# Eight W1 units started on two token tiles, with the other two tiles loaded through a transposing DMA

## The chip, the cores and the metric

One Trainium2 chip; the kernel runs on one of its cores. The metric is the device time of one execution in microseconds, as the median of several runs. A profiled execution beside them gives the span (first to last instruction), what every engine did, and when each DMA landed.

The engines are written as the profile writes them: PE (TensorE, matmul), PEld (its weight loads), ACT (ScalarE), DVE (VectorE), POOL (GpSimd) and SP (SyncE, which only issues DMAs here). ACT issues DMAs too.

## The reference

Two branches read the same input x (2048 tokens by 512) and are mixed by a gate. `B_x` is not used.

```
x = A_x
g = _sigmoid((x * gate_w).sum(-1, keepdims=True))

# A: linear attention, 32 heads of 16
qkv = x @ wqkv                                   # 512 -> 3 * 512
pq, pk = q @ w_phi, k @ w_phi                    # per head, 16 x 16
phi = concatenate([softmax(p), softmax(-p)])     # per head, 32 features
kv = einsum("bhsf,bhsd->bhfd", phi_k, v);  z = phi_k summed over the tokens
o  = (phi_q @ kv) / (phi_q . z + 1e-6)
a  = o @ wo

# B: dense layer with relu
b = maximum(x @ w1, 0) @ w2                      # 512 -> 1376 -> 512

return g * a + (1 - g) * b
```

## The kernel before

**Tiles.** The 2048 tokens are 16 tiles of 128, or four chunks of 512. The contraction over 512 is done in four row blocks j of 128. `XT` holds x transposed (features on the partitions), `W1` the first dense weight by row blocks, `HT` the hidden layer after the relu. The 1376 hidden columns are ten units of 128 and a rest of 96 which also carries the gate's column.

**Tasks and orders.** The program is a graph of named tasks. Each has an engine, a function that emits instructions, and the tasks that it waits for. The order of the tasks on each engine is written out by hand in the table `ORDER` (lines 17 to 62), one string for each engine; `schedule` only checks it. The numbers `dur`, `lat` and `boost` of a task are not used for the order. `settle` leaves out waits that others imply, and `emit` writes the instructions. Each DMA has a semaphore of its own.

The names that matter here:

- `x00` to `x03`: plain loads of the first four tiles of x, 128 KB each; `xt..` transposes one on PE against the identity (lines 382 to 391), two blocks at a time; `xe..` evicts the result from PSUM to `XT`, on ACT (L396) and DVE (L399).
- `w1a0` to `w1a3`: the columns 0 to 511 of W1, one row block each, 128 KB. `w1b`: columns 512 to 1023, all row blocks, 512 KB. `w1c`: the rest. All are issued at L306, on SP or ACT.
- `hh..`: the first four W1 units on tiles 0 and 1 (256 tokens), row block by row block, as the loads land (L439). `hr..` and the first `h0_0` to `h0_3`: the same units on tiles 2 and 3 (L445). Then `h0_4` and so on: a unit on a whole chunk of 512 tokens, four matmuls of 512 columns (L425).
- `rl..`: relu of a unit from PSUM into `HT`, on ACT (L503).
- `wphi`, `wbd..`, `wkT`, `f1_..` (L408), `fe1_..`: the head-wise map is folded into the key weight; the evictions `fe1_..` alternate between DVE (L378) and ACT (L376).
- `pr_k0` to `pr_k8` (L545): keys of two tiles at a time, features already mapped; `ev` (ACT, L577) evicts, `mx` and `mn` (DVE) reduce, `t1` and `t2` (POOL, L590) subtract, `ex` (ACT, L595) takes the exponential, `sm` and `rc` (DVE) sum and invert, `nm` (POOL, L604) normalises. `pr_q..` does the same for the queries (`ra` and `nm` on POOL, L623 and L627).
- `v..` (L526) and `kv..` (L611): the values, and phi_k times v summed over all tiles. `kv15` is the last one; `kn` and `kz` then evict the sum.
- `nd..` (L654), `to..`, `a..` (L682) and `b..` (L676): numerator and denominator, the transposed result, and the two output projections. Most of this fills the last third.
- `x1`, `x2`, `x3`, `wkT`, `wqT`: transposing loads (`load_t`, L311) on SP. `x1` waits until `w1c` has landed.
- `warm0`: six matmuls on constants at the start (L292).

PSUM has eight banks: 3, 4, 5 (`HB`) and 2 for the W1 units, 0, 1, 6 and 7 (`FB`) for the transposes, the folds, and later for other work. A bank's next user waits for its last eviction (`freed`).

Of the kernel before, what the change touches and what calls it, by code (L numbers as in the profile page):

```python
# [5 lines left out]
ACT = mybir.ActivationFunctionType  # L6
# [176 lines left out]
def bass_gated_mix__linear_kernel_hedgehog__dense_activation_relu__prompt_kernel(  # L183
# [38 lines left out]
    with ExitStack() as es:  # L222
# [157 lines left out]
        XB, FB = ((0, 1), (6, 7), (0, 1), (6, 7)), (0, 1, 6, 7)  # L380
# [7 lines left out]
        for m in range(4):  # L388
            for n in range(2):
                add(f"xt{m}{n}", "pe", lambda q, m=m, n=n: pe_xt(q, m, n),  # L390
                    (f"x0{m}", "ident", f"xe{m - 2}{n}" if m > 1 else None), dur=0.2, boost=9000.0 - 10 * m)
            for n, eng in enumerate(("act", "dve")):
                xo = XT[:, 2 * n:2 * n + 2, m * P:(m + 1) * P]
                xi = PS[:, XB[m][n], 0:2 * P].rearrange("p (j t) -> p j t", j=2)
                if eng == "act":
                    add(f"xe{m}{n}", eng, lambda q, o=xo, i=xi: q.activation(o, i, ACT.Copy), (f"xt{m}{n}",), dur=0.35,  # L396
                        boost=9000.0 - 10 * m)
# [15 lines left out]
        for c in range(NC):  # L413
            units += [("h", c, k) for k in range(KT - 1)]
# [5 lines left out]
        freed[FB[2]] = ("xe30",)  # L420
        w1of = {k: (() if k < 4 else ("w1b",) if k < 8 else ("w1c",)) for k in range(KT)}
# [15 lines left out]
        def pe_h_first(q, j, c0, c1, ks=range(4)):  # L437
            for k in ks:
                last = q.matmul(PS[:, GB4[k], c0:c1], W1[:, j, k * P:(k + 1) * P], XT[:, j, c0:c1],  # L439
# [3 lines left out]
        def pe_h_rest(q, k, c0, c1, first):  # L443
            for j in range(ND):
                last = q.matmul(PS[:, GB4[k], c0:c1], W1[:, j, k * P:(k + 1) * P], XT[:, j, c0:c1],  # L445
                                start=(j == 0 and first), stop=(j == ND - 1), skip_group_check=True)
# [7 lines left out]
        for n, (j, ks) in enumerate(((1, range(4)), (2, range(4)), (3, (0, 1)), (3, (2, 3)))):  # L454
            add(f"hh{n + 1}", "pe", lambda q, j=j, ks=ks: pe_h_first(q, j, 0, 2 * P, ks),
                (f"xe0{j // 2}", f"xe1{j // 2}", f"w1a{j}", prev), dur=0.11 * len(ks), boost=8500.0)
            prev = f"hh{n + 1}"

        for k in range(2):
            add(f"hr{k}", "pe", lambda q, k=k: pe_h_rest(q, k, 2 * P, 3 * P, True), ("xe20", "xe21", prev), dur=0.22,  # L460
                boost=8200.0)
            prev = f"hr{k}"
        for line in (("warm0", "xt00", "xt01", "xt10", "xt11", "hh00", "hh01", "hh1", "hh2", "xt20", "xt21", "hh3", "xt30", "xt31",
                      "hh4", "hr0", "hr1"), ("xe00", "xe10", "xe20", "xe30"),
                     ("ident", "shift", "xe01", "xe11", "xe21", "xe31", "blk", "row4", "mk")):
# [10 lines left out]
        for n, (kind, a, k) in enumerate(units):  # L476
            b = GB4[n] if n < 4 else FB[2] if n == 4 else HB[(n - 4) % len(HB)]
            if kind == "h":
                halved = n < 4
                deps = [*xof[a], *w1of[k], prev, *freed[b]]  # L480
                if k == KT - 1:
# [298 lines left out]
```

## Time and profile before

| what | us |
|---|---|
| median of 3 runs (150.11 to 150.15) | 150.13 |
| the profiled execution | 149.87 |
| its span | 148.3 |
| PE busy | 145.5 (98%) |
| DVE busy | 111.7 (75%) |
| POOL busy | 109.6 (74%) |
| ACT busy | 91.4 (62%) |

The share of busy time says who works, not who sets the end. For that the profile follows a chain back from the last instruction, at each step to what released it. A matmul's end is modelled, and matmuls overlap, so how fast PE works is read from the distance of their starts. For a DMA the profile gives the issue on the engine's queue and the time from the issue to the landing.

Landings of the early loads, issue and landing in us from the start of the span:

| load | issued | landed |
|---|---|---|
| x00 (SP), x01 (ACT) | 0.74, 0.74 | 3.45, 3.64 |
| w1a0 (SP), w1a1 (ACT) | 1.20, 1.18 | 4.12, 4.33 |
| w1a2 (SP), w1a3 (ACT) | 1.66, 1.67 | 4.83, 5.10 |
| x02, x03 (SP) | 2.13, 2.60 | 5.37, 5.68 |
| w1b, wphi (SP) | 3.08, 3.55 | 7.56, 7.79 |
| wkT, w1c, wv (SP) | 4.11, 7.43, 8.05 | 9.46, 11.54, 12.92 |

### The profile page before, as it was taken

The page shows a single profiled execution, that of the slowest core. Times are in us where ns is not written, and L with a number is a line of the kernel's source. Part 1 is how long each engine was busy: PE and PEld are TensorE (multiplying, and loading weights), DVE is VectorE, ACT ScalarE, POOL GpSimd, SP SyncE. Part 2 cuts the span into 40 slices and gives each one's busy share as a digit, 9 for nine tenths or more (in the row PEclk, how much of TensorE's full clock was granted, in tenths as well). Part 3 has the DMA queues.
Part 4 walks back from the last instruction along what each step waited for, and adds up shares of the span by engine and source line. Part 5 has one row for each costly group of instructions (what it writes and reads, how often), then busy time and mean ns, then how long its engine had stood idle before and what let it go on. Part 6 is the DMA issues. An engine that isn't in the chain of part 4 may idle for free.

```text
span 148.3 us, 2542 instructions
## 1 busy us (share of the span) xinstructions
PE 145.5 (98%) x1009; PEld 75.3 (51%) x1009; DVE 111.7 (75%) x169; ACT 91.4 (62%) x126; POOL 109.6 (74%) x72
## 2 busy tenths in 40 slices
PE   7999999999999999999999999999999999999994
PEld 2875444445654475445444545455444444445453
DVE  2433666998896948989999997999999988634502
ACT  3475769799969765898983937175583751310141
POOL 4000499999999999999999999999999793150000
PEclk9999999999999999999999999999999999999999
DMA  4998999910040001000000093646957785556752
GB/s 139 324 256 220 169 187 214 340 51 4 0 73 0 0 4 38 0 0 4 0 0 0 7 141 71 141 95 138 183 119 167 180 214 116 141 134 158 64 157 92
DMA packets 46363, 16.11 MB, mean 109 GB/s; under 512 B 39856, under 2 KB 46352, under 8 KB 46352
## 3 DMA queue, kind: packets, MB, share of 16 engines
q1 hardware_dynamic: 43760, 13.61, 42.6%
q10 hardware_dynamic: 2592, 2.34, 4.9%
q8 instruction: 8, 0.13, 0.4%
q14 instruction: 3, 0.02, 0.1%
HBM read 4.41 MB, written 2.10 MB: 44 GB/s over the span
## 4 chain that ended last, share of the span: by engine, by line
PE 98%; DVE 0%; issue 0%
PE PS L676 24%; PE PS L425 21%; PE PS L545 19%; PE PS L526 9%; PE PS L682 9%; PE PS L611 3%; PE PS L654 3%; PE PS L433 2%; PE PS L292 2%; PE PS L698 2%; PE PS L439 2%; PE PS L445 1%; PE PS L408 1%; PE PS L384 1%; PE PS L709 1%; DVE OSB L719 0%
## 5 line engine op out<-in xcount | busy, mean ns | idle before, releaser
L590 POOL TENSOR_TENSOR TS<-PB,MX 128x1024 bf16<-128x1024 bf16 (+1 forms) x18 | 30.9, 1723 | 14.5 <-DVE MX L581 14.5
L676 PE MATMUL PS<-W,HT 128*128 128x512 bf16 (+1 forms) x165 | 38.1, 379 | 0.0
L597 DVE TENSOR_REDUCE ZB<-FT 128x128 f32<-128x2048 bf16 (+1 forms) x18 | 36.6, 2031 | 1.8 <-ACT FT L595 1.8
L595 ACT ACTIVATE FT<-TS 128x2048 bf16<-128x2048 bf16 (+1 forms) x18 | 30.9, 1718 | 9.6 <-POOL TS L590 9.5
L425 PE MATMUL PS<-XT,W 128*128 128x512 bf16 x144 | 34.7, 379 | 0.0
L590 POOL TENSOR_TENSOR TS<-MN,PB 128x1024 bf16<-128x1024 bf16 (+1 forms) x18 | 30.9, 1726 | 0.8 <-DVE MN L583 0.8
L545 PE MATMUL PS<-WP,XT 128*128 128x512 bf16 x128 | 30.6, 379 | 0.0
L604 POOL TENSOR_TENSOR FT<-FT,SC 128x2048 bf16<-128x2048 bf16 (+1 forms) x9 | 29.6, 3293 | 0.0
L503 ACT ACTIVATE HT<-PS 128x512 bf16<-128x512 f32 x40 | 22.6, 597 | 5.4 <-PE PS L425 4.6
L581 DVE TENSOR_REDUCE MX<-PB 128x64 bf16<-128x1024 bf16 (+1 forms) x18 | 19.5, 1085 | 5.9 <-ACT PB L577 5.9
L676 PEld LDWEIGHTS PS<-W,HT 128*128 128x128 bf16 (+1 forms) x165 | 15.4, 98 | 16.9
L730 ACT ACTIVATE OSB<-PS,OMG 128x512 bf16<-128x512 f32 x14 | 9.6, 686 | 21.1 <-PE PS L682 20.5
L583 DVE TENSOR_REDUCE MN<-PB 128x64 bf16<-128x1024 bf16 (+1 forms) x18 | 19.3, 1084 | 3.2 <-ACT PB L577 3.2
L425 PEld LDWEIGHTS PS<-XT,W 128*128 128x128 bf16 x144 | 13.7, 98 | 15.4
L577 ACT ACTIVATE PB<-PS 128x1024 bf16<-128x1024 f32 (+1 forms) x18 | 16.7, 927 | 7.2 <-PE PS L545 4.0
L545 PEld LDWEIGHTS PS<-WP,XT 128*128 128x128 bf16 x128 | 12.1, 98 | 13.5
L526 PE MATMUL PS<-WV,XT 128*128 128x512 bf16 x64 | 16.4, 379 | 0.0
L627 POOL TENSOR_TENSOR FT<-FT,SR 128x1024 bf16<-128x1024 bf16 (+1 forms) x9 | 15.7, 1740 | 0.7
L682 PE MATMUL PS<-WO,OT 128*128 128x512 bf16 x60 | 14.9, 378 | 0.0
L663 DVE SCALAR_TENSOR_TENSOR OTM<-PS,EG,RD 128x256 bf16<-128x256 f32 x32 | 13.8, 463 | 0.2
L661 DVE RECIPROCAL RD<-PS 128x16 f32<-128x16 f32 x32 | 6.4, 232 | 9.0 <-PE PS L654 8.8
L535 ACT ACTIVATE VS<-PS 128x512 bf16<-128x512 f32 x16 | 9.6, 602 | 4.3 <-PE PS L526 4.3
(55 smaller groups left out, 106.6 us busy)
## 6 DMA issues: line engine op xcount, KB each, us to landing
out_dram<-OSB ACTq DMA_DIRECT2D x14, 128.0 KB, 2.2
W<-in_B_w_dram SPq DMA_DIRECT2D x1, 1280.0 KB, 7.5
W<-in_B_w_dram SPq DMA_DIRECT2D x1, 512.0 KB, 4.5
WV<-in_A_wqkv_dram SPq DMA_DIRECT2D x1, 512.0 KB, 4.9
WO<-in_A_wo_dram SPq DMA_DIRECT2D x1, 512.0 KB, 7.5
FT<-in_A_x_dram SPq DMA_DIRECT2D x3, 128.0 KB, 3.1
W<-in_B_w_dram SPq DMA_DIRECT2D x1, 352.0 KB, 4.1
W<-in_B_w_dram ACTq DMA_DIRECT2D x2, 128.0 KB, 3.3
```

The lines of the kernel that those rows point to most:

```text
L425: last = q.matmul(PS[:, b, :], W1[:, j, k * P:(k + 1) * P], XT[:, j, chunk(c)], start=(j == 0), stop=(j == ND - 1))
L503: add(f"rl{a}_{k}", "act", lambda q, a=a, k=k, b=b: q.activation(HT[:, k, chunk(a)], PS[:, b, :], ACT.Relu), (prev,), dur=0.6, boost=RL)
L526: last = q.matmul(PS[:, 2, :], XT[:, j, m * P:(m + 1) * P], WV[:, j, :], start=(j == 0), stop=(j == ND - 1))
L545: last = q.matmul(PS[:, n, :], XT[:, j, m * P:(m + 1) * P], WP[:, s, j, :], start=(j == 0), stop=(j == ND - 1))
L581: add(f"mx_{J}", "dve", lambda q, sl=sl, w=w, i=pbg: q.tensor_reduce(MX[:, sl, 0:w * H], i, AX.X, ALU.max), (f"ev_{J}", old("t1")), dur=0. ...
L583: add(f"mn_{J}", "dve", lambda q, sl=sl, w=w, i=pbg: q.tensor_reduce(MN[:, sl, 0:w * H], i, AX.X, ALU.min), (f"ev_{J}", old("t2")), dur=0. ...
L590: add(f"{tn}_{J}", "pool", lambda q, o3=o3, a3=a3, b3=b3: q.tensor_tensor(o3, a3, b3, ALU.subtract), (f"{'mx' if sg == 0 else 'mn'}_{J}", ...
L595: add(f"ex_{J}", "act", lambda q, fs=fs, ts=ts, w=w: q.activation(FT[:, fs, 0:w * F], TS[:, ts, 0:w * F], ACT.Exp), (f"t1_{J}", f"t2_{J}", ...
L597: add(f"sm_{J}", "dve", lambda q, fs=fs, sl=sl, w=w: q.tensor_reduce(ZB[:, sl, 0:2 * w * H], FT[:, fs, 0:w * F].rearrange("p (g d) -> p g ...
L604: add(f"nm_{J}", "pool", lambda q, f3=f3, sl=sl, w=w: q.tensor_tensor(f3, f3, SC[:, sl, 0:2 * w * H].unsqueeze(2).to_broadcast([P, 2 * w * ...
L676: last = q.matmul(PS[:, ab, :], HT[0:r, k, m * P:(m + 1) * P], W2[0:r, k, :], start=(k == 0), stop=False)
L682: last = q.matmul(PS[:, ab, :], OT[:, m % NOT, t, :], WO[:, t, :], start=False, stop=(t == ND - 1))
```

## The change

- Tiles 2 and 3 of x are no longer loaded plainly and transposed on PE. One transposing load, `x0b`, brings them straight into `XT`. It stands on SP behind `wphi` and ahead of `wkT`. The tasks `x02`, `x03`, `xt2.`, `xt3.`, `xe2.`, `xe3.` are gone.
- `w1b` is split into `w1b0` (row blocks 0 and 1, on SP, where `x02` was) and `w1b1` (row blocks 2 and 3, on ACT), 256 KB each.
- Eight W1 units, not four, are started on tiles 0 and 1, by row blocks: `hh00` to `hh3` for units 0 to 3 and `hg0` to `hg3` for units 4 to 7, in the banks 3, 4, 5, 2, 0, 1, 6, 7 (`GB8`). Their second halves (tiles 2 and 3) follow in the order 4 to 7, then 0 to 3, each four matmuls of 256 columns. The folds `f1_..` take banks 0, 1, 6, 7 and so wait for the relus of units 4 to 7.
- The relus of units 1, 5 and 7 of the first chunk go from ACT to DVE, as a maximum with 0.
- A small activation, `first`, stands on ACT between the issue of `x01` and that of `w1a1`.
- The orders on all engines are new up to about `kv15`; from there on they are the same.

```diff
-        load_x(0, "sp", 2.95)
-        load_x(1, "act", 3.1)
-        load_w(0, "sp", 3.2)
-        load_w(1, "act", 3.4)
-        load_w(2, "sp", 3.8)
-        load_w(3, "act", 3.95)
-        load_x(2, "sp", 4.0)
-        load_x(3, "sp", 3.9)
-        load("w1b", "sp", W1[:, :, 512:1024], w1r[:, :, 512:1024], dur=0.5, lat=5.0)
+        load_x(0, "sp", 2.95)
+        load_x(1, "act", 3.1)
+        add("first", "act", lambda q: q.activation(EP[:, 0:1], bass.AP(tensor=one, offset=0, ap=[[1, P], [1, 1]]), ACT.Copy),
+            (), dur=1.5)
+        after_last("first", "act")
+        for j in range(ND):
+            load(f"w1a{j}", ("sp", "act")[j % 2], W1[:, j, 0:512], w1r[:, j, 0:512], dur=0.45, lat=3.3)
+        for j in range(2):
+            load(f"w1b{j}", ("sp", "act")[j], W1[:, 2 * j:2 * j + 2, 512:1024], w1r[:, 2 * j:2 * j + 2, 512:1024], dur=0.45, lat=3.9)
         load("wphi", "sp", WPS[:, :, :], A_w_phi.rearrange("(g hl) r c -> (hl r) g c", g=ND), dur=0.5, lat=4.9)
+        load_t("x0b", XT[:, :, 2 * P:4 * P], x2[2 * P:4 * P, :], (), 1.3, 2.5)
         load_t("wkT", WT[:, ND:2 * ND, :], A_wqkv[:, D:2 * D], (), 4.1, 2.7)
...
-        def pe_h_rest(q, k, c0, c1, first):
+        def pe_h_rest(q, k, c0, c1):
             for j in range(ND):
-                last = q.matmul(PS[:, GB4[k], c0:c1], W1[:, j, k * P:(k + 1) * P], XT[:, j, c0:c1],
-                                start=(j == 0 and first), stop=(j == ND - 1), skip_group_check=True)
+                last = q.matmul(PS[:, GB8[k], c0:c1], W1[:, j, k * P:(k + 1) * P], XT[:, j, c0:c1],
+                                start=(j == 0), stop=(j == ND - 1), skip_group_check=True)
             return last
-        GB4 = (*HB, 2)
+        GB8 = (*HB, 2, *FB)
...
+        for j in range(1, ND):
+            add(f"hh{j}", "pe", lambda q, j=j: pe_h_first(q, j, 0, 2 * P),
+                (f"xe0{j // 2}", f"xe1{j // 2}", f"w1a{j}", prev), dur=0.44, boost=8500.0)
+            prev = f"hh{j}"
+        for j in range(ND):
+            add(f"hg{j}", "pe", lambda q, j=j: pe_h_first(q, j, 0, 2 * P, range(4, 8)),
+                ("xe00", "xe01", "xe10", "xe11", f"w1b{j // 2}", prev), dur=0.44, boost=8500.0)
+            prev = f"hg{j}"
...
+                if a == 0 and k in (1, 5, 7):
+                    add(f"rl{a}_{k}", "dve", lambda q, a=a, k=k, b=b: q.tensor_scalar(
+                        HT[:, k, chunk(a)], PS[:, b, :], 0.0, None, ALU.max), (prev,), dur=0.69, boost=RL)
+                else:
+                    add(f"rl{a}_{k}", "act", lambda q, a=a, k=k, b=b: q.activation(
+                        HT[:, k, chunk(a)], PS[:, b, :], ACT.Relu), (prev,), dur=0.6, boost=RL)
...
-            war = [f"xe{2 + j // 2}{j % 2}"] + (["rl0_4"] if j == 2 else [])
+            war = [f"rl0_{4 + j}"]
```

The new orders, up to the first key maximum on each engine, and on POOL and PE up to `nm_k8` and `kv15`:

```
sp    x00 w1a0 w1a2 w1b0 wphi x0b wkT w1c wv x1 x2 wqT x3 gw w2a w2b wo ...
act   x01 first w1a1 w1a3 w1b1 xe00 xe10 rl0_4 rl0_6 fe1_1 fe1_3 rl0_2 ev_k0 rl0_3 rl0_0 rl0_8 ...
dve   ident shift xe01 xe11 blk row4 wbd1 wbd3 mk wbd2 wbd0 rl0_5 rl0_7 fe1_0 fe1_2 rl0_1 mx_k0 ...
pe    warm0 xt00 xt01 xt10 xt11 hh00 hh01 hh1 hh2 hh3 hg0 hg1 hg2 hg3 h0_4 h0_5 h0_6 h0_7 h0_0
      f1_0 f1_1 f1_2 f1_3 h0_1 h0_2 pr_k0a pr_k0 h0_3 h0_8 h0_9 pr_k1 v0 h1_0 pr_k2 h1_1 h1_2 pr_k3 ...
      v15 h3_9 pr_q5 kv14 h3_10 kv15 b0 ...
pool  ... nm_k0 nm_k1 t2_k4 t1_k4 t1_k5 nm_k2 t2_k6 t1_k6 t2_k5 nm_k4 nm_k3 t2_k7 t1_k8 t2_k8 t1_k7
      t2_q0 nm_k5 t1_q0 nm_k6 t2_q1 t1_q1 ra_q0 nm_q0 nm_k7 nm_k8 ...
```

More of the change, by code (lines that the diff above doesn't have):

```diff
@@ L18 @@
     "sp": (
[3 rows of a table removed]
+        "x00 w1a0 w1a2 w1b0 wphi x0b wkT w1c wv x1 x2 wqT x3 gw w2a w2b wo hx0 hx1 hx2 tq0 tq1 hx3 to0 tq2 tq3 "
+        "to1 tq4 tq5 to2 to3 tq6 to4 tq7 to5 tq8 to6 tq9 to7 tq10 tq11 to8 to9 tq12 to10 tq13 tq14 to11 tq15 to12 "
+        "to13 to14 to15 st14 st15_1 "
     ),
     "pool": (
[4 rows of a table removed]
[4 rows of a table added]
     ),
     "act": (
[8 rows of a table removed]
[8 rows of a table added]
     ),
     "dve": (
[10 rows of a table removed]
[10 rows of a table added]
     ),
     "pe": (
[9 rows of a table removed]
[9 rows of a table added]
     ),
@@ L322, in load_x @@
             load(f"x0{m}", eng, XN[:, m, :], x0r[:, m, :], dur=0.45, lat=lat)
-        def load_w(j, eng, lat):
-            load(f"w1a{j}", eng, W1[:, j, 0:512], w1r[:, j, 0:512], dur=0.45, lat=lat)
         load_x(0, "sp", 2.95)
         load_x(1, "act", 3.1)
-        load_w(0, "sp", 3.2)
-        load_w(1, "act", 3.4)
-        load_w(2, "sp", 3.8)
-        load_w(3, "act", 3.95)
-        load_x(2, "sp", 4.0)
-        load_x(3, "sp", 3.9)
-        load("w1b", "sp", W1[:, :, 512:1024], w1r[:, :, 512:1024], dur=0.5, lat=5.0)
+        add("first", "act", lambda q: q.activation(EP[:, 0:1], bass.AP(tensor=one, offset=0, ap=[[1, P], [1, 1]]), ACT.Copy),
[5 more added lines that the diff above has]
+            load(f"w1b{j}", ("sp", "act")[j], W1[:, 2 * j:2 * j + 2, 512:1024], w1r[:, 2 * j:2 * j + 2, 512:1024], dur=0.45, lat=3.9)
         load("wphi", "sp", WPS[:, :, :], A_w_phi.rearrange("(g hl) r c -> (hl r) g c", g=ND), dur=0.5, lat=4.9)
+        load_t("x0b", XT[:, :, 2 * P:4 * P], x2[2 * P:4 * P, :], (), 1.3, 2.5)
         load_t("wkT", WT[:, ND:2 * ND, :], A_wqkv[:, D:2 * D], (), 4.1, 2.7)
@@ L378, in evict @@
                 add(name, eng, lambda q: q.tensor_copy(out_, PS[:, b, :]), deps, dur=0.69, **how)
-        XB, FB = ((0, 1), (6, 7), (0, 1), (6, 7)), (0, 1, 6, 7)
+        XB, FB = ((0, 1), (6, 7)), (0, 1, 6, 7)
         def pe_xt(q, m, n):
@@ L386, in pe_xt @@
             return last
-        for m in range(4):
+        for m in range(2):
             for n in range(2):
-                add(f"xt{m}{n}", "pe", lambda q, m=m, n=n: pe_xt(q, m, n),
-                    (f"x0{m}", "ident", f"xe{m - 2}{n}" if m > 1 else None), dur=0.2, boost=9000.0 - 10 * m)
+                add(f"xt{m}{n}", "pe", lambda q, m=m, n=n: pe_xt(q, m, n), (f"x0{m}", "ident"), dur=0.2,
+                    boost=9000.0 - 10 * m)
             for n, eng in enumerate(("act", "dve")):
@@ L400, in bass_gated_mix__linear_kernel_hedgehog__dense_activation_relu__prompt_kernel @@
                         boost=9000.0 - 10 * m)
-        x0 = [f"xe{m}{n}" for m in range(4) for n in range(2)]
+        x0 = [*(f"xe{m}{n}" for m in range(2) for n in range(2)), "x0b"]
         xof = [x0, ["x1"], ["x2"], ["x3"]]
@@ L413, in bass_gated_mix__linear_kernel_hedgehog__dense_activation_relu__prompt_kernel @@
         for c in range(NC):
-            units += [("h", c, k) for k in range(KT - 1)]
+            units += [("h", c, k) for k in ((4, 5, 6, 7, 0, 1, 2, 3, *range(8, KT - 1)) if c == 0 else range(KT - 1))]
             if c:
@@ L419, in bass_gated_mix__linear_kernel_hedgehog__dense_activation_relu__prompt_kernel @@
         freed = {b: () for b in (*HB, 2)}
-        freed[FB[2]] = ("xe30",)
-        w1of = {k: (() if k < 4 else ("w1b",) if k < 8 else ("w1c",)) for k in range(KT)}
+        w1of = {k: (() if k < 8 else ("w1c",)) for k in range(KT)}
         def pe_h(q, c, k, b):
@@ L438, in pe_h_first @@
             for k in ks:
-                last = q.matmul(PS[:, GB4[k], c0:c1], W1[:, j, k * P:(k + 1) * P], XT[:, j, c0:c1],
+                last = q.matmul(PS[:, GB8[k], c0:c1], W1[:, j, k * P:(k + 1) * P], XT[:, j, c0:c1],
                                 start=(j == 0 and c0 == 0), stop=(j == ND - 1), skip_group_check=True)
             return last
-        def pe_h_rest(q, k, c0, c1, first):
+        def pe_h_rest(q, k, c0, c1):
             for j in range(ND):
-                last = q.matmul(PS[:, GB4[k], c0:c1], W1[:, j, k * P:(k + 1) * P], XT[:, j, c0:c1],
-                                start=(j == 0 and first), stop=(j == ND - 1), skip_group_check=True)
+                last = q.matmul(PS[:, GB8[k], c0:c1], W1[:, j, k * P:(k + 1) * P], XT[:, j, c0:c1],
+                                start=(j == 0), stop=(j == ND - 1), skip_group_check=True)
             return last
-        GB4 = (*HB, 2)
+        GB8 = (*HB, 2, *FB)
         add("hh00", "pe", lambda q: pe_h_first(q, 0, 0, P), ("xe00", "w1a0"), dur=0.22, boost=8500.0)
@@ L453, in bass_gated_mix__linear_kernel_hedgehog__dense_activation_relu__prompt_kernel @@
         prev = "hh01"
[L454 to L465, printed above, removed]
+        for j in range(1, ND):
[6 more added lines that the diff above has]
+            prev = f"hg{j}"
+        for line in (("warm0", "xt00", "xt01", "xt10", "xt11", "hh00", "hh01", "hh1", "hh2", "hh3", "hg0", "hg1", "hg2", "hg3"), ("xe00", "xe10"),
+                     ("ident", "shift", "xe01", "xe11", "blk", "row4", "mk")):
             for a, b in zip(line, line[1:]):
@@ L476, in bass_gated_mix__linear_kernel_hedgehog__dense_activation_relu__prompt_kernel @@
         for n, (kind, a, k) in enumerate(units):
-            b = GB4[n] if n < 4 else FB[2] if n == 4 else HB[(n - 4) % len(HB)]
+            b = GB8[k] if n < 8 else HB[(n - 4) % len(HB)]
             if kind == "h":
-                halved = n < 4
-                deps = [*xof[a], *w1of[k], prev, *freed[b]]
+                halved = n < 8
+                deps = [*xof[a], *w1of[k], prev, *(() if halved else freed[b])]
                 if k == KT - 1:
@@ L498, in bass_gated_mix__linear_kernel_hedgehog__dense_activation_relu__prompt_kernel @@
                 add(f"h{a}_{k}", "pe", lambda q, a=a, k=k, b=b, h=halved:
-                    pe_h_rest(q, k, (3 if k < 2 else 2) * P, 4 * P, k > 1) if h else pe_h(q, a, k, b),
-                    deps, dur=(0.22 if k < 2 else 0.44) if halved else 0.87,
+                    pe_h_rest(q, k, 2 * P, 4 * P) if h else pe_h(q, a, k, b),
+                    deps, dur=0.44 if halved else 0.87,
                     boost=8000.0 if n < 3 else 0.0)
                 prev = f"h{a}_{k}"
-                add(f"rl{a}_{k}", "act", lambda q, a=a, k=k, b=b: q.activation(
-                    HT[:, k, chunk(a)], PS[:, b, :], ACT.Relu), (prev,), dur=0.6, boost=RL)
+                if a == 0 and k in (1, 5, 7):
[4 more added lines that the diff above has]
+                        HT[:, k, chunk(a)], PS[:, b, :], ACT.Relu), (prev,), dur=0.6, boost=RL)
                 freed[b] = (f"rl{a}_{k}",)
@@ L593, in bass_gated_mix__linear_kernel_hedgehog__dense_activation_relu__prompt_kernel @@
             if jn == NF - 2:
-                war += [f"xt{m}{n}" for m in range(4) for n in range(2)]
+                war += [f"xt{m}{n}" for m in range(2) for n in range(2)]
             add(f"ex_{J}", "act", lambda q, fs=fs, ts=ts, w=w: q.activation(
```

65 rows, old and new, of the table ORDER are left out of this document.

## The prediction

> **What bounds the kernel now.** I read the chain of waits first. It names one engine almost alone:
>
> ```profile
> span 148.3 us, 2542 instructions
> PE 98%; DVE 0%; issue 0%
> ```
>
> The chain starts with PE's first matmul at 0.77 us, and the 2% outside PE are that wait and the last eviction and store. So a saving counts only if it takes time out of PE's own sequence and no wait fills the hole. Next the start of the chain, in order of time (start, length, what):
>
> ```profile
> 0.77 2.72 PE PS L292 x6
> 3.49 0.09 issue
> 3.58 1.01 PE PS L384 x8
> 4.59 1.81 PE PS L439 x16
> 6.41 0.22 PE PS L384 x4
> 6.63 0.22 PE PS L439 x2
> 6.85 0.22 PE PS L384 x4
> 7.07 0.22 PE PS L439 x2
> 7.29 1.88 PE PS L445 x24
> 9.16 0.86 PE PS L425 x4
> ```
>
> Eight transposes (L384) cost 1.01 us at 3.58, four cost 0.22 at 6.41: between them PE's pace doubled. In the starts of single matmuls 128 columns go from 107 to 56 ns between 5.26 and 5.47 us (the granted clock reads 1.00 on both sides, so that row does not tell of it). After that PE issues a 256-column matmul every 109 ns and a 512-column one every 215.7 ns. Taking each start against this pace, I find one hole of more than 30 ns from 5.47 us to the end: 112 ns at 7.02, ahead of L445 (hr0 waits for the evictions of tile 2). Third, the timeline of the first 16 us, for the queues and ScalarE:
>
> ```profile
> 0.74 0.41 ACTq L306 DMA_DIRECT2D FT<-in_A_x_dram  x1
> 1.18 0.94 ACTq L306 DMA_DIRECT2D W<-in_B_w_dram  x2
> 2.13 0.91 SPq L306 DMA_DIRECT2D FT<-in_A_x_dram  x2
> 2.15 1.28 ACT L396 ACT_TABLE_LOAD   x1 [2.15 <-issue]
> 3.99 0.81 ACT L396 ACTIVATE XT<-PS 128x256 bf16<-128x256 f32 x2 [0.56 <-PE PS L384]
> 4.11 3.27 SPq L311 DMA_TRANSPOSE WT<-in_A_wqkv_dram  x1
> ```
>
> The table load lies behind ACT's DMA issues and ends at 3.43, before the first eviction is wanted. Last, the groups:
>
> ```profile
> L590 POOL TENSOR_TENSOR TS<-PB,MX 128x1024 bf16<-128x1024 bf16 (+1 forms) x18 | 30.9, 1723 | 14.5 <-DVE MX L581 14.5
> ```
>
> POOL idles 14.5 us once, until the first maximum; in the timeline it then runs without a gap from 16.77 to 116.28 us (0.08 us ahead of each nm_q apart). It is a second chain just behind PE's. PE takes POOL's last k result (nm_k8, ends 86.03) with kv15 at 86.50: 0.47 us in hand.
>
> **What the change takes out of PE.** Compare the stretch from the end of the sixteen L439 (6.41) to the first full unit (9.16). Before: 0.22 x 4 + 1.88 = 2.76 us; in it two tiles' transposes (0.44), the hole (0.11), and 2.2 us of L439 and L445. After: hh3, four 256-column matmuls, 0.44; hg0 to hg3, sixteen, 1.75; together 2.19. That is 0.57 less. Then the eight units' second halves, 32 x 109.2 ns = 3.49, against h0_4 to h0_7 whole, 16 x 215.7 ns = 3.45: 0.04 back. **Net -0.53 us.** The slow first part (before 5.4 us) is unchanged: it starts with the same x00, whose landing at 3.45 us releases PE at 3.58, and its 16 matmuls keep their form.
>
> **What must land in time.** With PE 0.5 us earlier, the needs in the new order are, from the same sums: hh1 at 5.26 (w1a1), hh3 at 6.25 (w1a3), hg0 at 6.7 (w1b0), hg2 at 7.55 (w1b1), h0_4 at 8.45 (x0b), f1_0 after five half units at 10.6 (wkT).
>
> - w1b0 is issued where x02 was (2.13 us). x02, 128 KB, landed 3.2 us after issue, w1b, 512 KB, 4.5 us: 256 KB lies between, 5.4 to 6.6. In time, by 0.1 us at the bad end. w1b1, if issued at 2.13 on ACT, is earlier than its need by 0.9.
> - x0b (256 KB, transposed) is issued on SP behind w1b0 and wphi, at 3.15. Nearest rows: L630's transposes of 256 KB land 2.8 us after issue, x1 of 512 KB 5.7: 5.95 to 8.85, need 8.45. I take 7.7: wkT landed at 9.46, x0b has half its bytes (its short packets ran from 6.6 to 8.85, so -1.15), and 0.22 MB less lies ahead of it, at the 0.37 MB/us of the DMA rows (-0.6). Bad end: 0.4 us of stall.
> - wkT goes one transposing load later, 7.7 + 2.3 = 10.0 against 10.6; before, it landed 1.3 ahead of f1_0. Behind it on SP all loads move by some 0.5 us: w1c 11.54 to 12.0 (h0_8 wants it at 14.6), and with it x1, which waits for w1c, 17.23 to 17.7 (h1_0 wants it near 18.9), then x2, wqT, x3, gw, w2 and wo, each with microseconds in hand.
> - ScalarE and VectorE: four evictions of 0.38 to 0.43 us go; rl0_1, rl0_5 and rl0_7 move to VectorE, at some 0.65 us (its 512-column cast L378 takes 0.69), in a stretch where it idles 2.29 and 3.03 us. Were that cover gone, f1_1 and f1_3 would wait for rl0_5 and rl0_7, which end some 0.5 us before.
>
> **The step I weigh most: `first`.** It puts an activation, and with it the 1.28 us table load, between x01 and w1a1 on ACT. Queued behind it are w1a1, w1a3 and w1b1, and PE waits for all three. The trace has no DMA issue behind a table load, so I bound it. Lower end, nothing: ACT's queue issued a store at 106.30 us while the 0.69 us activation that began at 106.30 still ran, so issuing does not wait for the engine. Upper end, load and activation in full: issue at 1.18 + 1.28 + 0.2 (a small activation, L471, takes 0.19) = 2.66, landing 2.7 to 3.4 later (fastest and slowest row of 128 KB) at 5.4 to 6.1, so hh1 stalls 0.1 to 0.8, and xe00 comes 0.1 later. I take the lower end: the row of 106.30 is the same queue with work running on the same engine.
>
> The Trainium skill speaks against it: "ScalarE: Activation LUTs", section "What ACT_TABLE_LOAD costs", counts 1283 ns for the load, which the trace has, plus 1380 ns of drain, 2.66 us a switch. By it w1a1 is issued near 3.8 and the sum is the third rival's; the trace shows no drain beside the one table load.
>
> **The later order.** All of PE's work after that is kept, re-sorted up to kv15; its last third is untouched. I walked the new orders with the rows' durations at the closest points. pr_k0 ends 5.68 us after hg3 (1.75 + 0.44 + 0.89 for f1 + 0.87 + 1.73), at 14.1 instead of 14.38, so POOL starts 0.25 us earlier while PE gained 0.53: at kv15 0.2 us are left of 0.47. POOL itself has new tight places (nm_k4 now ahead of nm_k3, so ahead of it VectorE's sm_k4 and rc_k4; t2_q0 behind mn_k8, rc_k5, mn_q0), where I get 0 to 0.2 us each. PE's next closest are pr_k2 and pr_k3 behind ev_k1 and ev_k2 (0.5 us before) and h1_5 behind rl1_2 with some 0.25. I charge 0.06; ends 0 and 0.5.
>
> **Sum:** -0.53 + 0.06 = -0.47 us. The profiled execution took 149.87 (span 148.3 and 1.6 around it): 149.40. The median of the runs is 150.13, 0.26 above it; on that scale **149.66 us**.
>
> **Rivals.**
> 1. *ACT's queue is held by the table load, once* (25%). For: w1a1, w1a3 and w1b1 stand behind it in one queue. Against: 106.30. hh1 waits till 5.75, the middle; later needs move along and are met. -0.47 + 0.45 = **150.1**, no change; the point at which the gain is gone is a landing at 5.73.
> 2. *The orders lose their slack* (13%). A late VectorE result opens holes in POOL, and kv15, then every nd behind kn and kz, waits. POOL must lose over 0.25 + 0.47 = 0.7 us against now to make the kernel slower, 1.2 us gives **150.6**. For: 0.47 is all there is in hand now. Against: POOL lost nothing from 16.77 on before, and most waits I walked keep 0.3 us or more.
> 3. *The queue is held for load and drain* (7%), the slower side. Place: w1a1's issue. Price by rows: two lengths of 1.28, issue at 3.75, landing 6.5 to 7.2, stall 1.2 to 1.9, so +0.7 to +1.5, **151.2**. It decides once w1a1 is issued after 2.9 us (landing past 6.0). It would also leave PE idle where its pace doubles (5.3 us). A later doubling would cost up to 27 matmuls at 213 instead of 109 ns.
> 4. *The transposing load is late* (10%): the change does not free PE because x0b, and wkT behind it, land at the bad ends. 0.4 to 0.6 of stall: **150.1**, 150.4 at worst.
>
> The Trainium skill, "TensorE: Matmul & The Clock Gate", Part 1, makes the doubling a matter of a busy window of about 3.4 us that runs freely and not from the kernel's start. By it a stall shorter than a window, like rival 1's, costs only itself; the trace agrees so far as PE was busy 4.6 us before the doubling.
>
> **Chances.** The forecast holds 45%, its own range 149.45 to 149.85. About 0.2% (0.3 us) is what a measurement of this kernel can tell from no change. Faster by more: nearly all of the forecast and a quarter of rival 1, with scraps, 0.50. Slower: rival 3, most of 2, parts of 1 and 4: 0.26. Within: 0.24. The range 149.35 to 150.70 takes in the forecast, rival 1, rival 4 and half of rival 2, and leaves out rival 3 and the tails, under 2 in 10.
>
> **What would show it.** Chain: two groups of L384 gone, no "issue" or hole between 4.6 and 12 us, the first whole W1 unit behind f1. Timeline: the two W loads on ACT's queue starting at 1.2 (forecast) or 2.5 to 2.7 (rival 1) or 3.8 (rival 3). DMA rows: the transposing x load landing before 8.4. POOL: its 14.5 us idle about 0.25 shorter and no new idle groups; kv15 (L611) near 86.0. The forecast is wrong if hh1 (L439 in the new file) starts after 5.5 us, or if PE has holes of over 0.2 us past 9 us.

## The result, and the profile after

| | before | after |
|---|---|---|
| median us | 150.11 (149.97 to 150.15, 6 runs) | 150.75 (150.33 to 150.93, 6 runs) |
| ratio to before, 95% interval | | 1.0041 [1.0028, 1.0054] |
| the profiled execution, its span | 149.87, 148.3 | 150.93, 149.4 |
| landing of w1b (before); w1b0, w1b1 (after) | 7.56 | 7.83, 8.06 |
| landing of w1a1, w1a2, w1a3 | 4.33, 4.83, 5.10 | 4.32, 5.26, 5.43 |
| landing of x0b; of wkT | none; 9.46 | 9.32; 11.07 |

The change makes the kernel 0.41% slower; 149.66 was forecast, and the time lies just past the upper end of the range, 150.70. The page of the changed kernel names other work on the chain than before (PE 98%):

```profile
span 149.4 us, 2539 instructions
PE 84%; DVE 9%; DMA 4%; issue 1%; SPq 1%
```

DMA's 4% is one piece of 5.7 us at the start; DVE's 9% lies between 90.4 and 104.3 us and is taken up under orders_tail. The same chain in order of time (start, length, what):

```profile
2.08 0.04 issue
2.13 5.70 DMA W<-in_B_w_dram
7.83 0.05 issue
7.87 1.92 PE PS L436 x16
9.79 2.18 PE PS L442 x20
11.97 0.89 PE PS L406 x16
```

The transfer that starts at 2.13 is w1b0. PE's hg0 to hg3 (L436) wait for it and start at 7.87. By its own pace PE was ready for them at 6.71, where 6.7 was forecast. Before, the chain was PE's alone from 0.77. Three other views show the same wait, PE's timeline (idle time before the group in brackets), the waits of PE from 5 to 110 us (in total, times, longest), and the DMA rows (KB, time from issue to landing) of w1b0 and w1b1:

```profile
7.87 1.92 PE L436 MATMUL PS<-XT,W 128*128 128x256 bf16 x16 [1.00 <-DMA W<-in_B_w_dram]
...
PE PS L436 <- DMA W<-in_B_w_dram: 1.0, 1, 1.0
...
W<-in_B_w_dram SPq DMA_DIRECT2D x1, 256.0 KB, 5.7
W<-in_B_w_dram ACTq DMA_DIRECT2D x1, 256.0 KB, 5.9
```

The idle time is 1.0 with modelled ends of matmuls; by the distance of the starts the hole is 1.16. The four loads w1a of 128 KB took 2.9 to 3.8 us from issue to landing, so twice the bytes cost some 2 us more here.

ScalarE's start, from the timeline:

```profile
0.73 0.41 ACTq L306 DMA_DIRECT2D FT<-in_A_x_dram  x1
1.18 1.28 ACT L326 ACT_TABLE_LOAD   x1 [1.18 <-PEq L765]
1.24 1.36 ACTq L306 DMA_DIRECT2D W<-in_B_w_dram  x3
```

The table load runs from 1.18 to 2.46, and w1a1, w1a3 and w1b1 are issued from 1.24 on, beside it. POOL's idle time, 14.5 before, has grown although PE's part of the work has become shorter:

```profile
L590 POOL TENSOR_TENSOR TS<-PB,MX 128x1024 bf16<-128x1024 bf16 (+1 forms) x18 | 30.9, 1721 | 15.7 <-DVE MX L581 15.6
```

**Where the time went.** I split PE's time by the starts of its matmuls: the time at full pace, what the half pace at the start costs on top, and the holes (all that is over the pace).

| us | before | after | difference |
|---|---|---|---|
| PE's first transpose | 3.58 | 3.62 | +0.04 |
| half pace, on top | 0.66 | 0.66 | 0 |
| work at full pace | 140.79 | 140.37 | -0.42 |
| holes | 1.12 | 2.61 | +1.49 |

That is +1.11, the difference of the spans (149.44 - 148.33). The holes: +1.16 ahead of hg0, +0.25 ahead of nd4_0 at 104.35, +0.13 ahead of kv15 at 87.30, -0.11 at 7.02 (gone with hr0), +0.06 in small ones.

### The profile page after: what moved, and what is told of

Its sections match the earlier page's. It is cut to its first block, busy times and chain, and to the rows that moved or that the text cites. A ratio compares the mean times of both kernels' runs of the same rounds, so it can differ in the third digit from the quotient of the medians.

```text
span 149.4 us, 2539 instructions
## 1 busy us (share of the span) xinstructions
PE 145.5 (97%) x1009; PEld 76.3 (51%) x1009; DVE 113.1 (76%) x170; ACT 88.9 (59%) x122; POOL 109.6 (73%) x72
## 4 chain that ended last, share of the span: by engine, by line
PE 84%; DVE 9%; DMA 4%; issue 1%; SPq 1%
PE PS L422 18%; PE PS L676 17%; PE PS L545 17%; PE PS L526 9%; PE PS L682 8%; DMA W<-in_B_w_dram 4%; DVE ZB L597 3%; PE PS L611 3%; DVE OTM L663 2%; PE PS L442 2%; PE PS L654 2%; PE PS L430 2%; PE PS L698 2%; PE PS L436 1%; PE PS L406 1%
## 5 line engine op out<-in xcount | busy, mean ns | idle before, releaser
L590 POOL TENSOR_TENSOR TS<-PB,MX 128x1024 bf16<-128x1024 bf16 (+1 forms) x18 | 30.9, 1721 | 15.7 <-DVE MX L581 15.6
L597 DVE TENSOR_REDUCE ZB<-FT 128x128 f32<-128x2048 bf16 (+1 forms) x18 | 36.6, 2031 | 0.7 <-ACT FT L595 0.7
L422 PE MATMUL PS<-XT,W 128*128 128x512 bf16 x128 | 30.7, 379 | 0.0
L503 ACT ACTIVATE HT<-PS 128x512 bf16<-128x512 f32 x37 | 20.9, 601 | 9.9 <-PE PS L442 5.9
L583 DVE TENSOR_REDUCE MN<-PB 128x64 bf16<-128x1024 bf16 (+1 forms) x18 | 19.3, 1082 | 1.1 <-ACT PB L577 1.1
L422 PEld LDWEIGHTS PS<-XT,W 128*128 128x128 bf16 x128 | 12.1, 98 | 13.2
L663 DVE SCALAR_TENSOR_TENSOR OTM<-PS,EG,RD 128x256 bf16<-128x256 f32 x32 | 14.0, 464 | 0.4
```

Of the source, the lines that this page charges most:

```text
L422: last = q.matmul(PS[:, b, :], W1[:, j, k * P:(k + 1) * P], XT[:, j, chunk(c)], start=(j == 0), stop=(j == ND - 1))
L503: add(f"rl{a}_{k}", "act", lambda q, a=a, k=k, b=b: q.activation(HT[:, k, chunk(a)], PS[:, b, :], ACT.Relu), (prev,), dur=0.6, boost=RL)
L583: add(f"mn_{J}", "dve", lambda q, sl=sl, w=w, i=pbg: q.tensor_reduce(MN[:, sl, 0:w * H], i, AX.X, ALU.min), (f"ev_{J}", old("t2")), dur=0. ...
L590: add(f"{tn}_{J}", "pool", lambda q, o3=o3, a3=a3, b3=b3: q.tensor_tensor(o3, a3, b3, ALU.subtract), (f"{'mx' if sg == 0 else 'mn'}_{J}", ...
L597: add(f"sm_{J}", "dve", lambda q, fs=fs, sl=sl, w=w: q.tensor_reduce(ZB[:, sl, 0:2 * w * H], FT[:, fs, 0:w * F].rearrange("p (g d) -> p g ...
```

## The experiments

Two questions were open: why w1b0 is 1.2 us later than its bound, and what the later orders cost. Holes and landings below are from one profiled execution of each kernel, medians and ratios from all its runs beside runs of the kernel before.

**x0b_plain.** Does the transposing load, whose packets are on the same DMA engines, hold w1b0 up? The same 256 KB, loaded plainly (the kernel leaves out the transposition of tiles 2 and 3):

```diff
-        load_t("x0b", XT[:, :, 2 * P:4 * P], x2[2 * P:4 * P, :], (), 1.3, 2.5)
+        load("x0b", "sp", XT[:, :, 2 * P:4 * P], x2[2 * P:4 * P, :].rearrange("(p q) d -> p (q d)", q=2).rearrange("p (j b) -> p j b", b=2 * P), dur=0.45, lat=4.0)
```

> Tiles 2 and 3 enter by a plain load of the same 256 KB in the same place of SP's queue, untransposed, so the output for them is not the reference's; all else as in the changed kernel. Theory A (crossing): w1b0 landed at 7.83 us because the short packets of the transposing load ran on the DMA engines among the plain packets of w1b1 from ACT's queue. Then here w1b0 and w1b1 land by 6.8, the hole ahead of hg0 shrinks from 1.16 to under 0.2 us, and the time is 149.6 to 149.9. Theory B (amount): eight plain loads from two queues are simply through no earlier; w1b0 lands at 7.5 or later also here, the hole stays over 0.9 and the time is 150.5 to 150.9.

Measured: 150.66 us (149.87 to 151.25, 10 runs), ratio 1.0024 [1.0003, 1.0044]. w1b0 landed at 7.64, w1b1 at 7.84, w1a2 at 6.28; PE waited 0.64 ahead of hh2 and 0.38 ahead of hg0. The loads are as late without x0b's transposition (wkT's, issued at 3.80, is still behind them): the theory of crossing packets has lost its main ground, and the next run takes both away.

**x0b_waits.** The same question from the other side: x0b is issued only after both halves of w1b have landed.

```diff
-        load_t("x0b", XT[:, :, 2 * P:4 * P], x2[2 * P:4 * P, :], (), 1.3, 2.5)
+        load_t("x0b", XT[:, :, 2 * P:4 * P], x2[2 * P:4 * P, :], ("w1b0", "w1b1"), 1.3, 2.5)
```

> The transposing load x0b waits on SP until w1b0 and w1b1 have landed. Theory A: w1b0 and w1b1 land by 6.8, hg0 starts within 0.2 us of hh3's end; but x0b is issued at some 6.8 and lands near 10.5 to 11, so PE stalls ahead of h0_4 for 2 us, and wkT and all behind it come later too: 151.5 to 152.5. Theory B: w1b0 lands at 7.5 or later, x0b near 11.5, time 152.5 or more.

Measured: 152.88 us (152.7 to 153.27, 4 runs), ratio 1.0182 [1.0162, 1.0201]. Its chain:

```profile
2.14 5.86 DMA W<-in_B_w_dram
...
8.08 1.31 SPq L311
9.39 0.05 issue
9.44 4.73 DMA WT<-in_A_wqkv_dram
```

The first line is w1b1, issued on ACT and landed at 8.00, w1b0 at 7.80, with nothing transposing in flight. x0b is issued at 8.08 and lands at 11.64, wkT at 14.17: x0b's wait costs 2.09 us ahead of h0_4 and 0.42 ahead of the folds. w1b0 is as late as in the changed kernel, so theory A, the crossing packets, falls.

This trace also says what "late" means. A load's semaphore goes up in sixteen steps, and PE waits for the last. Half of w1b0's shares had landed at 5.91, fifteen at 6.59, the last at 7.80; from 6.2 to 7.8 all DMA together moved 17, 9, 9 and 3 KB in steps of 0.4 us. One share held the load. The Trainium skill, "DMA: Bandwidth & Descriptors", section "Why a DMA increments its semaphore by 16 and not by 1", has the sixteen steps as the sixteen DMA engines that finish independently, of which only the full count means landed, and its section "Queues, rings and completion order" lets each engine take turns between the queues that have work for it. The steps seen here agree with the first; the second is put to the test next, and the turns themselves are shown behind the table of all profiles.

**w1b1_on_sp.** w1b1 goes from ACT's queue to SP's, behind w1b0, so that nothing of the second half can take turns with the first.

```diff
-        "x00 w1a0 w1a2 w1b0 wphi x0b ...
+        "x00 w1a0 w1a2 w1b0 w1b1 wphi x0b ...
...
-            load(f"w1b{j}", ("sp", "act")[j], W1[:, 2 * j:2 * j + 2, 512:1024], ...
+            load(f"w1b{j}", "sp", W1[:, 2 * j:2 * j + 2, 512:1024], ...
```

> w1b1 is issued on SP right behind w1b0, so that the transposing load stands behind all plain loads in one queue; ACT keeps x01, w1a1, w1a3. Theory A: no crossing, w1b0 lands by 6.2, w1b1 by 7.3, x0b near 8 to 8.4, hole ahead of hg0 gone; time 149.6 to 149.9. Theory B: w1b0 comes earlier as it no longer shares with w1b1, but w1b1 lands near 7.8 to 8.1 as before, a hole of 0.3 to 0.6 ahead of hg2; time 150.1 to 150.5.

Measured: 150.07 us (149.52 to 150.35, 12 runs), ratio 0.9989 [0.9975, 1.0003], apart from the changed kernel's 1.0041 [1.0028, 1.0054]. The move also put w1b1's issue from 2.15 to 2.60; two queues with this later issue were not run. Its chain:

```profile
3.49 1.00 PE PS L382 x8
4.50 4.42 PE PS L436 x36
8.92 2.18 PE PS L442 x20
```

All of hh and hg run in one piece: w1b0 landed at 6.59 and w1b1 at 7.32. The holes at kv15 (0.13, at 86.43) and nd4_0 (0.25, at 103.48) are still there.

**no_first.** The changed kernel without `first`; the table load goes back behind ACT's issues.

```diff
-        "x01 first w1a1 w1a3 w1b1 ...
+        "x01 w1a1 w1a3 w1b1 ...
```

> Without the activation first, so the table load comes behind ACT's four DMA issues, from 2.6 to 3.9 us. Theory A and B: first does nothing to w1b0's landing (7.5 to 8.1), the hole stays near 1.1, time 150.6 to 150.9. Theory C (the table load slows the loads around 2.6 us, where 100 KB were moved in 0.4 us against 149 KB before): the loads run at some 149 KB in 0.4 us from 2.6 on, w1b0 lands by 7.2, time under 150.4.

Measured: 150.69 us (149.74 to 151.4, 10 runs), ratio 1.0033 [1.001, 1.0056], not to be told from the changed kernel. In its profile w1b0 landed at 6.70, in time. But its half pace lasted longer, to 6.4 us (1.34 us on top, 0.66 in the changed kernel), so PE came to hg0 later. The table load gives no time and takes none that these runs can show. Theory C has the landing it forecast (6.70), but not its reason: from 2.6 to 3.0 us 99 KB were moved here, and in kernels with `first` anything from 98 (x0b_waits) to 144 KB (orders_tail).

**before_again.** The kernel before, unchanged and profiled once more: are shares spread there too?

> The kernel before, unchanged, profiled once more. Theory S (one late share): on each load one or two of the sixteen shares come a microsecond behind the rest in any kernel, and before the cover was the distance to the need: w1b's last share here lands 7.5 to 8.5, its shares spread by 0.5 us or more also on w1a2, and PE still has no hole over 0.2 us, since w1b is wanted at 9.0. Theory K (the changed kernel's own doing): the shares of w1a2, x02 and x03 land within 0.3 us of each other as in the first profile, w1b by 7.6.

Measured: 150.19 us (149.8 to 150.66, 10 runs), ratio 1.001 [0.9993, 1.0028]. Its chain:

```profile
1.65 4.28 DMA W<-in_B_w_dram
5.93 0.14 issue
6.07 0.60 PE PS L439 x4
...
7.55 1.88 PE PS L445 x24
9.43 1.73 PE PS L425 x8
```

This time w1a2 landed at 5.93 (4.83 in the first profile) and is on the chain, with a hole of 0.31; w1b landed at 8.49 (7.56). Before that PE waited 0.70 us, until 4.88, in the end for w1a0, whose last share came at 4.75, 0.81 behind the fifteenth; theory S had no hole over 0.2. The spread is there without the change. w1b was 0.93 us later and cost nothing, because h0_4 wants it only at 9.43: x's transposes and the first units on tiles 2 and 3 lay between. The change took that work out and moved the need to 6.7.

**orders_tail.** The changed kernel, with the old order from `kn1` to `sm_q3` on DVE and from `b0` to `b1` on PE.

```diff
-        ... sm_q1 kn0 rc_q1 kn1 kz1 kz0 go0 rd0_0 gr3 ... mn_q4 rd1_1 ... mn_q5 sm_q3 ...
+        ... sm_q1 kn1 kn0 kz0 kz1 rc_q1 mn_q4 gr3 go0 ... mn_q5 rd2_0 rd2_1 o2_0 o2_1 sm_q3 ...
...
-        ... kv15 b0 nd0_1 nd0_0 b3 nd1_1 nd1_0 b2 pr_q6 nd2_1 nd2_0 a0 b1 ...
+        ... kv15 b0 nd0_0 nd0_1 b3 nd1_0 nd1_1 b2 pr_q6 a0 nd2_0 nd2_1 b1 ...
```

> The changed kernel with the old order of VectorE from kn1 to sm_q3 and of PE from b0 to b1; the loads untouched. Theory S says that the loads cost what they cost (hole ahead of hg0 0.2 to 1.4 us) and that the later orders add 0.38 of their own: the hole of 0.25 us ahead of nd4_0 near 104 goes, the one of 0.13 ahead of kv15 stays, and the time is 0.2 to 0.3 below the changed kernel's, 150.3 to 150.6. The rival, that both later holes are only an echo of the late start, has them unchanged and the time at 150.6 to 150.9.

Measured: 150.3 us (150.05 to 151.03, 12 runs), ratio 1.0019 [1.0, 1.0039]. The 0.25 ahead of nd4_0 is gone and 0.13 ahead of nd2 (97.52) has come: 0.12 in the holes. The ratios differ by 0.22%, with intervals that overlap. kv15's 0.13 stays. In the changed kernel's chain nd4_0 (L654) is released by DVE's `o3` (L663):

```profile
103.60 0.70 DVE OTM L663 x2
104.30 0.05 issue
104.35 0.30 PE PS L654 x4
```

Why `o3` was late is seen on DVE's timeline there, where `mn_q5` (L583) stands behind `o2` and so just ahead of `sm_q3` (L597), and `o3` behind both:

```profile
99.51 1.21 DVE L583 TENSOR_REDUCE MN<-PB 128x64 bf16<-128x1024 bf16 x1
100.64 2.28 DVE L597 TENSOR_REDUCE ZB<-FT 128x128 f32<-128x2048 bf16 x1
102.83 0.36 DVE L661 RECIPROCAL RD<-PS 128x16 f32<-128x16 f32 x2
103.10 0.49 DVE L621 RECIPROCAL SC<-ZB 128x64 f32<-128x64 f32 x1
103.52 0.78 DVE L663 SCALAR_TENSOR_TENSOR OTM<-PS,EG,RD 128x256 bf16<-128x256 f32 x2
```

and in the kernel before, where `mn_q5` comes ahead of `o2`, at 96.50:

```profile
96.50 1.21 DVE L583 TENSOR_REDUCE MN<-PB 128x64 bf16<-128x1024 bf16 x1
...
98.69 2.28 DVE L597 TENSOR_REDUCE ZB<-FT 128x128 f32<-128x2048 bf16 x1
...
101.58 0.78 DVE L663 SCALAR_TENSOR_TENSOR OTM<-PS,EG,RD 128x256 bf16<-128x256 f32 x2
```

PE is 1.11 us later in the changed kernel, DVE's `o3` 1.94.

**sp_tail** joins the two edits, w1b1 on SP and the old later order.

> w1b1 on SP behind w1b0, and the old later orders of VectorE and PE. If the two add up: 150.07 of the run with w1b1 on SP less 0.25, so 149.7 to 149.95, holes only ahead of kv15 (0.13) and at most 0.3 around w1a2 and w1b0. If the later holes are an echo: 150.0 to 150.15.

Measured: 149.69 us (149.27 to 150.05, 12 runs), ratio 0.9978 [0.9964, 0.9992]. w1b0 at 6.62 and w1b1 at 7.32 are in time; of waits on loads, 0.55 us ahead of hh2 (w1a2, 5.81) and 0.05 ahead of h0_4 (x0b, 8.56) are left. It differs from orders_tail in w1b1's queue alone, and the two ratios are apart: the second pair that shows the same.

**sp_tail_k1** also takes `pr_k1` ahead of `h0_9` on PE and `ev_k1` ahead of `rl0_9` on ACT, for the gap of 0.10 that POOL had ahead of t1_k1.

```diff
-        ... rl0_8 rl0_9 ev_k1 ...
+        ... rl0_8 ev_k1 rl0_9 ...
...
-        ... h0_8 h0_9 pr_k1 v0 ...
+        ... h0_8 pr_k1 h0_9 v0 ...
```

> As the run before it, and pr_k1 one unit earlier on PE (ahead of h0_9), ev_k1 ahead of rl0_9 on ACT. If kv15's hole comes from POOL's gap of 0.10 us ahead of t1_k1, that gap goes and the hole with it: 0.1 below the run before it, 149.6 to 149.85. If not, the hole of 0.13 ahead of kv15 stays and the time is the same.

Measured: 149.62 us (149.18 to 149.84, 12 runs), ratio 0.9963 [0.9948, 0.9978]: faster than both kernels. POOL's gap at t1_k1 went, one of 0.08 ahead of nm_k0 came, and the 0.13 at kv15 stayed, so that edit's reason is not shown. Its chain:

```profile
1.65 4.17 DMA W<-in_B_w_dram
...
5.95 2.78 PE PS L435 x24
8.73 2.27 PE PS L441 x20
11.00 0.89 PE PS L405 x16
```

w1a2, landed at 5.82, has taken w1b0's place: 0.81 us ahead of hh2. From there to the folds PE waits for nothing but 0.08 for x0b.

**w1a3_on_sp.** If turns between queues made w1b0 late, the same cure should help w1a2. To sp_tail_k1:

```diff
-        "x00 w1a0 w1a2 w1b0 w1b1 ...
+        "x00 w1a0 w1a2 w1a3 w1b0 w1b1 ...
...
-        "x01 first w1a1 w1a3 xe00 ...
+        "x01 first w1a1 xe00 ...
```

> sp_tail_k1 with w1a3 moved from ACT's queue to SP's, behind w1a2 and ahead of w1b0; ACT's queue keeps x01 and w1a1 alone. In sp_tail_k1 w1a2 landed at 5.82 us and PE had a hole of 0.81 us ahead of it; w1b0 was in time. Theory Q (a load's last share is late because a load of another queue stands beside it on each DMA engine): w1a2, with nothing but SP's own loads behind it, lands at 5.3 us or earlier, the hole ahead of it falls to 0.3 us or less, w1b0 is issued one step of 0.45 us later and lands near 7.0, still within 0.3 us of its need: 149.2 to 149.6 us. Rival S (the last share is late whatever stands beside it): w1a2 again at 5.6 to 6.0 and its hole again 0.5 to 0.8, w1b0 later on top: 149.7 to 150.2 us.

Measured: 149.98 us (149.54 to 150.22, 12 runs), ratio 0.9995 [0.9982, 1.0008]: slower than sp_tail_k1, not faster (its profiled execution, 149.70, is one of its faster ones, so the profile shows only a part of this). The landings went as theory Q has it: w1a2 at 5.05, and its hole fell from 0.81 to 0.04. But PE then came to hg0 earlier, w1b0 landed at 6.64 as ever, for 0.59, and x0b, issued 0.48 later behind one more load, put itself at the head of the chain, for 0.24:

```profile
4.10 4.54 DMA XT<-in_A_x_dram
8.64 0.05 issue
8.68 2.36 PE PS L441 x20
```

The wait was handed on from load to load: that one load comes early does not help while w1b0 lands at 6.6 and x0b at 8.6.

**w1b_whole.** sp_tail_k1 with w1b as one load of 512 KB in w1b0's place on SP.

```diff
-        for j in range(2):
-            load(f"w1b{j}", "sp", W1[:, 2 * j:2 * j + 2, 512:1024], ...
+        load("w1b", "sp", W1[:, :, 512:1024], w1r[:, :, 512:1024], dur=0.5, lat=4.5)
...
-                ("xe00", "xe01", "xe10", "xe11", f"w1b{j // 2}", prev), ...
+                ("xe00", "xe01", "xe10", "xe11", "w1b", prev), ...
```

> sp_tail_k1 with w1b0 and w1b1 loaded as one load of 512 KB on SP, issued where w1b0 was, so that all of hg0 to hg3 wait for the whole. It tells what the split itself is worth once one queue has both halves. If the queue's order is what serves w1b0 early (theory Q and the volume ahead of it): the whole lands where w1b1 did, 7.2 to 7.5 us, PE has a hole of 0.5 to 0.8 us ahead of hg0, 150.0 to 150.3 us. If halves land no earlier than a whole would (the split is worth nothing): w1b lands at 6.6 to 6.8 and the time is that of sp_tail_k1, 149.5 to 149.8 us.

Measured: 150.63 us (150.27 to 150.75, 11 runs), ratio 1.0032 [1.0019, 1.0045]. The split is worth 0.7% once one queue has both halves; more than expected, since the whole landed at 7.76 and not at 7.2 to 7.5. The hole is 0.42 ahead of hg0; another of 1.10 ahead of hh2 (w1a2, 6.38) lies before it and adds nothing, as hg0 had to wait for 7.76 in any case. Its chain looks like the changed kernel's:

```profile
2.13 5.64 DMA W<-in_B_w_dram
7.76 0.05 issue
7.81 1.92 PE PS L434 x16
9.73 2.18 PE PS L440 x20
```

A split whose second half travels beside the first (7.83) lands as late as no split at all (7.76).

**The changed kernel and its variants together**: landings of shares in us (8th, then the last), from the semaphore steps in the trace, and the time between the last shares of w1a2 and of w1b0 (w1b).

| kernel | w1a2 | w1b0, or w1b whole | between the last two |
|---|---|---|---|
| two queues: after | 4.70, 5.26 | 5.90, 7.83 | 2.57 |
| x0b_plain | 4.74, 6.28 | 5.90, 7.64 | 1.36 |
| x0b_waits | 4.62, 6.31 | 5.91, 7.80 | 1.49 |
| no_first | 4.57, 5.54 | 5.95, 6.70 | 1.16 |
| orders_tail | 4.64, 6.03 | 6.57, 7.42 | 1.39 |
| one queue: w1b1_on_sp | 4.76, 5.83 | 5.85, 6.59 | 0.76 |
| sp_tail | 4.83, 5.81 | 5.69, 6.62 | 0.81 |
| sp_tail_k1 | 4.72, 5.82 | 5.84, 6.64 | 0.82 |
| w1a3_on_sp | 4.40, 5.05 | 5.73, 6.64 | 1.59 |
| w1b_whole | 4.63, 6.38 | 6.55, 7.76 | 1.38 |

Half of the shares land alike in both arrangements, near 5.9 (orders_tail 6.57); the last ones differ: 6.70 to 7.83 in two queues, 6.59 to 6.64 in one. How w1b1 holds w1b0 up can be read from the packets of x0b_waits once a single engine is still at work. From 6.6 to 7.4 us its DMA row, in slices of 20 ns, has one packet at a time, as many from SP's queue (q1) as from ACT's (q10):

```profile
DMA  0100101010101010101010010101010101010100
...
q1 hardware_dynamic: 9, 0.01, 3.2%
q10 hardware_dynamic: 9, 0.01, 3.2%
```

In the records of the single packets they come strictly in turn, 1 KB of w1b0 and 1 KB of w1b1, one every 42 ns, from 6.51 to 7.44: eleven of each, so w1b1 took 0.47 us out of w1b0's last 0.93. The turns of which the Trainium skill tells in "Queues, rings and completion order" are there; it has them by whole packets of some 9 to 17 descriptors, where each turn here is one record of 1 KB.

So w1b1's place in ACT's queue is shown to cost time by two pairs of kernels, and the turns are seen at work in one. They are not the whole of it: two queues were in time once (no_first, 6.70), w1b0 came no earlier in w1a3_on_sp, where w1a2 did, and the turns of x0b_waits explain 0.47 us, not why that engine was behind the fifteen others. A candidate for the rest are single slow packets: a record of 1 KB takes 46 ns as a rule, but one in the changed kernel took 880 ns, at 5.32. The records do not name the engine, so this is not shown.

## Why the prediction was wrong

**The cut of PE's work was right.** Forecast: -0.42 at full pace and -0.11 for the hole at 7.02. Measured: -0.42 (140.79 to 140.37), and the hole is gone.

**`first` was right, and with it the choice between its ends.** ACT's issues run beside the table load (1.24 against 1.18), hh1 had w1a1 at 4.32 for a need of 5.26. Rivals 1 and 3 did not happen. The Trainium skill, "ScalarE: Activation LUTs", section "What ACT_TABLE_LOAD costs", counts 1380 ns of drain beside the load; here the load follows ACT's issue of x01 (0.73 to 1.14) at 1.18, and the activation behind it started at 2.47, 0.01 after it, so no run here shows the drain.

**The step that failed is "w1b0 ... 5.4 to 6.6. In time, by 0.1 us at the bad end".** It landed at 7.83. The bound was an interpolation by size between two loads of one profile, in which the shares of each load happened to lie within 0.3 us from the 8th to the last. It left out two things that the runs then showed. First, a load is as late as its slowest share, and that varies: the kernel before had w1a2 at 4.83 in one profile and 5.93 in the next. Second, the change puts the two halves into two queues, and w1b1 then takes turns with w1b0 on the engines: 6.70 to 7.83 in two queues, 6.59 to 6.64 in one. I had taken w1b1's earlier issue on ACT as a gain of 0.9 us on its need, and not as a cost to w1b0. The row of w1b, 512 KB in 4.5 us, was no upper end: 1.16 us was the price.

**x0b and wkT**: x0b at 9.32 is past its bound of 8.85, but so was PE, and it cost nothing in the changed kernel. Rival 4 named the wrong load. In sp_tail_k1, where PE is early again, x0b lands at 8.60, inside its bounds, and costs 0.08.

**The later order**: 0.06 was charged, 0 to 0.5 bounded, and 0.38 measured (0.25 + 0.13). The 0.25 lies where the prediction says "its last third is untouched", and the description of the change says that the orders past kv15 are the same. They are not: DVE's order differs up to `sm_q3` and PE's up to `b1`, as the diff shows, and nd4_0 waits just there. kv15's 0.13 is rival 2 in small. kv15 waits for POOL's nm_k8, which ended at 87.24, and of the 0.2 us that the prediction left in hand nothing was there. It has pr_k0 end at 14.1 instead of 14.38, but 14.1 is counted by the starts of matmuls and 14.38 by modelled ends; by starts pr_k0 ended at 14.21 before (12.48 + 1.73), so the gain was 0.1 and not 0.25. The traces bear it out: from pr_k0's first matmul to the point where it is ready for kv15 PE takes 73.59 us in the changed kernel and 74.02 before, 0.43 less, while POOL from its first subtraction to the end of nm_k8 takes 69.38 and 69.26, 0.12 more (a gap of 0.10 ahead of t1_k1). Together that is 0.55, more than the 0.47 in hand, and kv15 starts 0.06 after nm_k8's end: a hole of 0.13. POOL's later start (idle 15.7, not 14.5) is mostly w1b0's delay passed on, as pr_k0 hangs behind hg3. The old later order lies behind this hole and could not remove it; the earlier pr_k1 only traded one gap of POOL for another.

**The sum with the terms as measured**: -0.42 - 0.11 + 0.04 + 1.16 + 0.38 + 0.06 = +1.11 in the profiles. Without w1b0's term it is -0.05: as the change stands, the later orders would have used up nearly all of the gain.

**What stays open**: which engine has the last share and why it lags by up to 1.3 us in one profile and by 0.1 in another; and how much of the 2.57 us in the changed kernel's profile are turns.

## What to carry to other kernels

A load is in time when its slowest share is, so bound a landing from several profiles, and ask of a change not only when a load is issued but how far its need moves toward it: the kernel before had the same late loads, with 1.88 us of other work (L445) ahead of the need. Splitting a load to get its first half early paid here only with the second half behind it in the same queue: the same two halves gave 1.0041 in two queues and 0.9989 in one. Compare times on one scale: 14.1 by starts against 14.38 by modelled ends made a margin of 0.2 us that was not there. When a wait on a load is removed, look for the next load in the chain before counting the gain; w1a3_on_sp cured one hole of 0.81 and got two of 0.59 and 0.24.

## What the hardware showed unexpectedly

- PE's pace doubles at very different times in kernels with the same start: the last matmul at half pace began at 5.26 and 4.02 in two profiles of the kernel before, at 6.39 in no_first, and before the first transpose (3.44) in sp_tail_k1. That is up to 1.34 us of PE's time, though the granted clock reads 1.00 in all of them. An early doubling buys little here: sp_tail_k1 lost nothing to the half pace and then waited 0.81 us for w1a2.
- The sixteen shares of one 128 KB load can land within 0.15 us after the 8th (w1a2 before: 4.68, 4.83) or 1.75 us apart (w1b_whole: 4.63, 6.38).
- With loads of two queues on one engine, the packets go in turn, 1 KB from each, one every 42 ns (x0b_waits, 6.51 to 7.44).
- DMAs are issued on ACT's queue while its engine loads a table: w1a1 at 1.24, during the load from 1.18 to 2.46.
